# Linear attention's feature map: max(x, 0) + 1e-6 taken from PSUM behind the exp, min(exp, 1) added from SBUF

## The chip, the cores and the metric

The kernel runs on one core of a Trainium2 chip. The time is the device time of one execution in microseconds; the profiled execution has a span (first to last instruction) and its own time, which is a little longer. The core has five engines that run their own instruction streams and meet at semaphores: TensorE (PE), VectorE (DVE), ScalarE (ACT), GpSimd (POOL) and SyncE (SP, which issues DMAs here). Matmul results land in PSUM, in eight banks of 128 x 512 fp32; everything else lies in SBUF.

## The reference

Two blocks work on inputs of the same shapes (2048 tokens, 640 features, 32 heads of 20), and their outputs stand side by side. A is softmax attention, B linear attention:

```python
    def _A_ref(x, wqkv, wo):
        ...
        scores = jnp.einsum("bhqd,bhkd->bhqk", q, k) * (Dh ** -0.5)
        p = _softmax(scores, axis=-1)
        o = jnp.einsum("bhqk,bhkd->bhqd", p, v)
        ...
    def _B_ref(x, wqkv, wo):
        ...
        phi = lambda t: jnp.where(t > 0, t + 1, jnp.exp(t)) + 1e-6
        pq, pk = phi(q), phi(k)
        kv = jnp.einsum("bhsd,bhse->bhde", pk, v)
        z = jnp.einsum("bhsd->bhd", pk)
        num = jnp.einsum("bhqd,bhde->bhqe", pq, kv)
        den = jnp.einsum("bhqd,bhd->bhq", pq, z)[..., None] + 1e-6
        o = num / den
        ...
```

The feature map phi is the place of the change. It is computed as max(t, 0) + min(exp(t), 1) + 1e-6, which is the same for both signs of t.

## The kernel before

A is the large part. For each of 32 pairs of a query block (512 tokens) and a group of four heads, and each key tile of 128 tokens, PE makes the scores of four heads (matmuls `ps<-f_Qr,f_KT`), the exponential of them goes to SBUF, and PE multiplies it with V (`ps<-f_PT,f_V`). Most exponentials are ACT's: L1968 takes two PSUM banks at once (128 x 1024), 726 times. The others DVE makes in another way: L1828 clamps and rounds a bank to int16 (`f_Sr`), whose bits are read as bf16; POOL shifts them twice with INT64_ADD (L2039), and PE multiplies the three versions with V (`ps<-f_Sr,f_V` and `ps<-f_Sr,f_Vp`). PSUM bank 7 collects A's products with V; banks 1 to 4 take the scores for ACT in two pairs; the three auxiliary banks 0, 5 and 6 take everything else, DVE's scores and all of B.

B and the projections are put between A's work. B has two halves: for every 512 tokens K's features, V and their products (`kstep`, `vstep`, `kvstep`), then, behind a "turn", Q's features, the quotients and the output projection (`qstep`, `ndstep`, `trstep`, `ostep`). K's and Q's features come from `phi`, five banks per 512 tokens each, so 40 calls in all.

`phi` takes one auxiliary bank `b` with 512 columns. ACT writes exp of it to one of two SBUF buffers (`r1`, L1467); DVE does min(r1, 1) + 1e-6 in place (L1469), and then max(bank, 0) + r1 to the destination (L1471). Only after this is the bank given back (`self.abank.append(b)`). The exp of the next call but one waits for the same buffer.

The order of the instructions is no order of the source. A planner written in Python runs when the kernel is built: every engine has a clock, every operation a cost from a small formula (for DVE `_c_dve(n)` = 1.042 n + 68 ns, for L1469 0.95 n + 110), and what is ready first by these clocks is put into the engine's stream. On the chip each engine then runs its own stream in that fixed order and waits on semaphores where the data isn't ready. B's steps are paced by the share of A's exponentials that are placed. A change of a cost, or of the point at which a bank is given back, therefore moves instructions everywhere behind it.

Two more rules matter. An operation that reads a PSUM bank is booked as if it wrote it, so two readers of a bank follow each other (`op`, L118). And `turn` makes ACT and DVE wait, before Q's features begin, for everything that still uses buffers of the first half.

Of the kernel before, what the change touches and what calls it, by code (L numbers as in the profile page):

```python
# [7 lines left out]
BF16 = mybir.dt.bfloat16  # L8
# [4 lines left out]
ALU = mybir.AluOpType  # L13
# [730 lines left out]
def _c_dve(n):  # L744
    return 1.042 * n + 68
# [6 lines left out]
def _c_act(n):  # L752
    return 0.8333 * n + 50
# [27 lines left out]
class _Fast:  # L781
# [119 lines left out]
    def alloc(self):  # L901
        S, NT, NQC = self.S, self.NT, self.NQC
        self.KT = self.sb("f_KT", [128, N_GRP, S], BF16)
        self.V = self.sb("f_V", [128, NT, N_HEADS, 21], BF16)
        self.Vp = self.sb("f_Vp", [128, len(self.DKT), N_HEADS, 21], BF16)
        self.xT = self.sb("f_xT", [128, N_DC, S], BF16)
        self.wqp = self.sb("f_wqp", [128, _NP, N_DC, 128], BF16)
        zt = self.sb("f_zt", [128, 128], BF16)
        self.zt = zt[:]
        self.zr = zt[:].unsqueeze(1).broadcast_to([128, 2, 128])  # L910
        self.wq = self.sb("f_wq", [128, N_DC, D_MODEL], BF16)
        ar = self.sb("f_ar", [128, 20480], BF16)
        self.ar = ar
        nw = N_DC * D_MODEL
        self.wk = ar[:, 0:nw].rearrange("p (c n) -> p c n", c=N_DC)
        self.wv = ar[:, nw:2 * nw].rearrange("p (c n) -> p c n", c=N_DC)
        self.wB = ar[:, 0:2 * nw].rearrange("p (c n) -> p c n", c=N_DC)
        o = 2 * nw
        self.pk = ar[:, o:o + 2560].rearrange("p (t n) -> p t n", t=4)
        self.o = ar[:, o:o + 1280].rearrange("p (t n) -> p t n", t=2)  # L920
        self.oT = [ar[:, o + 1280 + 640 * k:o + 1920 + 640 * k] for k in range(2)]
        self.va = ar[:, o + 2560:o + 5248].rearrange("p (t h j) -> p t h j", t=4, j=21)
        self.pqT = ar[:, o + 2560:o + 5120].rearrange("p (c s) -> p c s", c=N_DC)
        o += 5248
        self.kvm = ar[:, o:o + 840].rearrange("p (c n) -> p c n", c=N_DC)
        self.kvacc = ar[:, o + 840:o + 2520].bitcast(F32).rearrange("p (c n) -> p c n", c=N_DC)
        self.oT += [ar[:, o + 840 + 640 * k:o + 1480 + 640 * k] for k in range(2)]
        self.wst0 = ar[:, o + 2432:o + 3712].rearrange("p (k c n) -> p k c n", k=2, c=N_DC)
        self.xn = ar[:, 2 * nw:2 * nw + 12 * D_MODEL].rearrange("p (t n) -> p t n", t=12)
        ee = ar[:, o + 2520:o + 2520 + 1024].rearrange("p (k n) -> p k n", k=2)  # L930
        self.er = {320: ee, 512: ee}
        o += 3712
        self.wkp = ar[:, o:o + 640 * _NP].rearrange("p (g c m) -> p g c m", g=_NP, c=N_DC)
        self.kq = [ar[:, o + 640 + 2048 * k:o + 640 + 2048 * (k + 1)] for k in range(2)]
        self.xB = [ar[:, o + k * 2560:o + (k + 1) * 2560].rearrange("p (c s) -> p c s", c=N_DC) for k in range(2)]
        assert o + 5120 <= 20480
        self.wo = self.sb("f_wo", [128, 7, D_MODEL], BF16)
        self.sq = self.sb("f_sq", [128, self.NSQ, 512], BF16)
        self.Qr = self.sb("f_Qr", [128, 4, 512], BF16)
        self.PT = self.sb("f_PT", [128, self.NPT, 512], BF16)  # L940
        self.xs = self.PT[:].rearrange("p t n -> p (t n)")[:, 4096:4096 + 4 * D_MODEL].rearrange("p (t n) -> p t n", t=4)
        self.Sr = self.sb("f_Sr", [128, self.NS, 4, 512], I16)
        self.T2 = self.sb("f_T2", [128, 512], BF16)
        self.OTn = self.sb("f_OTn", [128, 3 + self.NX, 512], BF16)
        self.OTd = self.sb("f_OTd", [128, 5, 512], BF16)
        self.Rt = self.sb("f_Rt", [128, 16 * self.NN], F32)
        self.stage = self.sb("f_st", [128, 4, 512], BF16)
        self.rd = self.sb("f_rd", [128, 2, 2, 24], F32)
        self.ident = self.sb("f_id", [128, 128], BF16)
        sm = self.sb("f_sm", [128, 8], F32)  # L950
        self.kb, self.km, self.gm = (sm[:, 2 * k:2 * k + 2] for k in range(3))
        self.warm, self.ones = sm[:, 6:7], sm[:, 7:8]
        self.kb16 = self.sb("f_kb16", [128, 2], BF16)
        self.g2 = self.sb("f_g2", [1, 2], F32)
        self.flag = self.sb("f_flag", [1, 1], I32)
        xf = self.xT[:].rearrange("p c s -> p (c s)")
        self.gt = xf[:, 5120:5120 + 4 * 1024].bitcast(F32).rearrange("p (k n) -> p k n", k=2)
# [498 lines left out]
    def phi(self, b, n, dst, res, key, extra=()):  # L1456
        k = self.brr % 2
        self.brr += 1
        src = self.ps[:, b, 0:n]
        r1 = self.er[n][:, k, 0:n]  # L1460
        rk = ("r1", n, k)
        prev = self.eru.get(k)
        self.eru[k] = key

        def ok():
            return prev is None or prev in self.done
        self.push("act", lambda e: e.activation(r1, src, AF.Exp), (("ps", b),), (rk,), _c_act(n), prio=0, ok=ok,  # L1467
                  after=lambda: self.push(
                      "dve", lambda e: e.tensor_scalar(r1, r1, 1.0, 1e-6, op0=ALU.min, op1=ALU.add), (rk,), (rk,),  # L1469
                      0.95 * n + 110, prio=0, after=lambda: self.push(  # L1470
                          "dve", lambda e: e.scalar_tensor_tensor(dst, src, 0.0, r1, op0=ALU.max, op1=ALU.add),  # L1471
                          (("ps", b), rk) + tuple(extra), (res,), _c_dve(n), prio=self.P5,
                          after=lambda: (self.done.add(key), self.abank.append(b)))))

    def b_steps(self):
        ps = self.ps
        sch = self.sch
# [123 lines left out]
        out.append(_Step(None, second, needs=allk, key="ld2"))  # L1601

        def turn(b):
            sch.barrier(("act", "dve"), tuple(("r1", 320, k) for k in range(2))
                        + tuple(("kva", c) for c in range(N_DC))
                        + tuple(("va", q) for q in range(6)) + tuple(("pk", q) for q in range(5)) + ("va1",))
        out.append(_Step(None, turn, needs=tuple(("kvm", c) for c in range(N_DC)), key="turn"))

        def qstep(tc, c, slot, needs):
# [886 lines left out]
```

## Time and profile before

| | |
|---|---|
| median of 3 runs | 718.65 us (718.63 to 719.19) |
| profiled execution | 718.41 us |
| its span | 716.7 us |
| granted TensorE clock, mean | 0.999 |

The page and the answers of the trace share their columns. A row of a group has the line, the engine, the operation, out<-in with shapes and the count; behind the bar stand the busy time of the group in us and the mean duration in ns; behind the second bar how long the engine was idle just before such an instruction, and what ended it. Since successive instructions of an engine overlap a little, the mean duration is longer than the step from one to the next. A row of the timeline begins with start and duration in us. Buffer numbers are left out of names. All of the planner's matmuls have one line, L166, that of the helper. `f_ar` is one large SBUF arena in which B's weights, inputs, K's and Q's features and the buffers r1 lie; `f_tt` is new with the change.

### The profile page before, as it was taken

The page shows a single profiled execution, that of the slowest core. Times are in us where ns is not written, and L with a number is a line of the kernel's source. Part 1 is how long each engine was busy: PE and PEld are TensorE (multiplying, and loading weights), DVE is VectorE, ACT ScalarE, POOL GpSimd, SP SyncE. Part 2 cuts the span into 40 slices and gives each one's busy share as a digit, 9 for nine tenths or more (in the row PEclk, how much of TensorE's full clock was granted, in tenths as well). Part 3 has the DMA queues.
Part 4 walks back from the last instruction along what each step waited for, and adds up shares of the span by engine and source line. Part 5 has one row for each costly group of instructions (what it writes and reads, how often), then busy time and mean ns, then how long its engine had stood idle before and what let it go on. Part 6 is the DMA issues. An engine that isn't in the chain of part 4 may idle for free.

```text
span 716.7 us, 25639 instructions
## 1 busy us (share of the span) xinstructions
PE 701.6 (98%) x11221; PEld 240.8 (34%) x11221; DVE 612.6 (85%) x1103; ACT 692.5 (97%) x774; POOL 329.7 (46%) x329
## 2 busy tenths in 40 slices
PE   8999999999899999999999999999999999999997
PEld 5423333333223333333332333333232333333333
DVE  6988888888888888887989887898888888999992
ACT  4789999999999999999999999999999999999996
POOL 6644354454535554245453357432444434444452
PEclk9999999999999999999999999999999999999999
DMA  9601010101340012011000112301020110010001
GB/s 267 105 18 36 12 31 9 40 12 30 88 100 7 22 33 60 10 24 35 7 11 10 34 25 71 78 14 36 8 55 25 47 28 6 26 28 7 28 16 39
DMA packets 46554, 27.59 MB, mean 38 GB/s; under 512 B 30842, under 2 KB 45882, under 8 KB 46442
## 3 DMA queue, kind: packets, MB, share of 16 engines
q1 hardware_dynamic: 43818, 23.98, 14.0%
q10 hardware_dynamic: 2624, 1.97, 0.9%
q8 instruction: 88, 1.44, 0.8%
q14 instruction: 24, 0.20, 0.1%
HBM read 8.40 MB, written 5.24 MB: 19 GB/s over the span
## 4 chain that ended last, share of the span: by engine, by line
ACT 58%; PE 36%; DVE 3%; POOL 2%; DMA 1%; issue 0%; ACTq 0%; DVEq 0%
ACT f_PT L1968 56%; PE ps L166 36%; POOL f_KT L1167 2%; ACT f_ar L1467 2%; DVE f_Sr L1828 1%; DMA f_ar<-in_A_wqkv_dram 1%; POOL f_V L1145 0%; DVE ps L2085 0%; PE ps L1046 0%; DVE f_ar L1471 0%; DVE f_PT L1419 0%; DVE f_ar L1469 0%; POOL f_Sr L2039 0%; DVE ps L2070 0%; DVE f_OTn L2079 0%
## 5 line engine op out<-in xcount | busy, mean ns | idle before, releaser
L1968 ACT ACTIVATE f_PT<-ps 128x1024 bf16<-128x1024 f32 x726 | 675.7, 1094 | 13.0 <-PE ps L166 12.3
L2039 POOL INT64_ADD f_Sr<-f_Sr x298 | 306.4, 1042 | 371.7 <-PE ps L166 343.1
L1828 DVE TENSOR_SCALAR f_Sr<-ps 128x512 int16<-128x512 f32 x596 | 402.2, 684 | 70.6 <-PE ps L166 64.2
L166 PE MATMUL ps<-f_Qr,f_KT 32*128 32x512 bf16 x2048 | 286.8, 384 | 7.3 <-ACT f_PT L1968 6.1
L166 PEld LDWEIGHTS ps<-f_Qr,f_KT 32*128 32x128 bf16 x2048 | 72.0, 91 | 256.2 <-ACT f_PT L1968 233.4
L166 PE MATMUL ps<-f_ar 128*32 128x512 bf16 (+6 forms) x3024 | 144.6, 295 | 0.7 <-DVE f_Sr L1828 0.3
L166 PE MATMUL ps<-f_PT,f_V 128*21 128x512 bf16 x1452 | 135.1, 383 | 0.1
L166 PE MATMUL ps<-f_Sr,f_V 128*21 128x512 bf16 x1192 | 106.9, 382 | 0.8 <-DVE f_T L2089 0.4
L166 PEld LDWEIGHTS ps<-f_ar 128*32 128x32 bf16 x3024 | 56.4, 95 | 58.0 <-issue 34.6
L166 PE MATMUL ps<-f_Sr,f_Vp 128*21 128x512 bf16 x596 | 57.5, 382 | 0.0
L166 PEld LDWEIGHTS ps<-f_PT,f_V 128*21 128x21 bf16 x1452 | 33.6, 90 | 46.2 <-issue 39.7
L166 PEld LDWEIGHTS ps<-f_Sr,f_V 128*21 128x21 bf16 x1192 | 26.5, 90 | 34.0 <-issue 24.7
L166 PE MATMUL ps<-f_ar,f_xT 128*32 128x160 bf16 x1280 | 34.8, 234 | 0.0
L166 PE MATMUL ps<-f_xT,f_ar 128*32 128x512 bf16 x400 | 30.8, 383 | 0.0
L166 PE MATMUL ps<-f_wo,f_OTd 128*32 128x512 bf16 (+5 forms) x608 | 30.6, 302 | 0.0
L166 PEld LDWEIGHTS ps<-f_ar,f_xT 128*32 128x32 bf16 x1280 | 22.8, 96 | 13.6 <-issue 9.5
L1471 DVE SCALAR_TENSOR_TENSOR f_ar<-ps,f_ar 128x512 bf16<-128x512 f32 x40 | 26.8, 671 | 0.2
L1467 ACT ACTIVATE f_ar<-ps 128x512 bf16<-128x512 f32 x40 | 26.5, 663 | 0.0
L1026 DVE CAST f_st<-ps 128x512 bf16<-128x512 f32 x35 | 23.9, 682 | 1.2 <-PE ps L166 0.9
L166 PE MATMUL ps<-f_xT,f_wq 128*32 128x512 bf16 x320 | 24.9, 383 | 0.0
L1469 DVE TENSOR_SCALAR f_ar<-f_ar 128x512 bf16<-128x512 bf16 x40 | 20.4, 509 | 3.7 <-ACT f_ar L1467 2.4
L2085 DVE STREAM_TRANSPOSE ps<-ps 128x512 f32<-128x512 f32 x31 | 22.4, 723 | 0.3 <-PE ps L166 0.2
(76 smaller groups left out, 278.2 us busy)
## 6 DMA issues: line engine op xcount, KB each, us to landing
out_dram<-f_st SPq DMA_DIRECT2D x35, 128.0 KB
f_ar<-in_B_wqkv_dram SPq DMA_DIRECT2D x15, 160.0 KB
f_OTd<-f_OTn SPq DMA_DIRECT2D x105, 20.0 KB
f_Qr<-f_sq SPq DMA_DIRECT2D x88, 20.0 KB
f_KT<-f_ar SPq DMA_DIRECT2D x22, 80.0 KB
f_ar<-in_A_wqkv_dram SPq DMA_DIRECT2D x1, 800.0 KB
f_ar<-in_A_wqkv_dram ACTq DMA_DIRECT2D x1, 800.0 KB
f_wq<-in_A_wqkv_dram ACTq DMA_DIRECT2D x1, 800.0 KB
```

The source lines that it names most:

```text
L166: lambda e: e.matmul(out, lhsT, rhs, start=start, stop=stop, tile_position=tp, skip_group_check=sgc),
L1026: (lambda e: e.tensor_copy(sl, ps[:, b, 0:w])), (("ps", b),), (res,),
L1167: self.push("pool", lambda e, g=g: e.tensor_copy(self.KT[:, g, :], self.kb16[:, 1:2].broadcast_to([128, self.S])), ("kb16",), tuple(("K", ...
L1467: self.push("act", lambda e: e.activation(r1, src, AF.Exp), (("ps", b),), (rk,), _c_act(n), prio=0, ok=ok, after=lambda: self.push("dve", ...
L1469: "dve", lambda e: e.tensor_scalar(r1, r1, 1.0, 1e-6, op0=ALU.min, op1=ALU.add), (rk,), (rk,),
L1471: "dve", lambda e: e.scalar_tensor_tensor(dst, src, 0.0, r1, op0=ALU.max, op1=ALU.add),
L1828: post = lambda: self.push("dve", lambda e: e.tensor_scalar(self.Sr[:, s, i, :], self.ps[:, b, :], 0.0, 32639.0 - self.PH[-1], op0=ALU.max ...
L1968: return _Op("act", lambda e: e.activation(self.PT[:, s0:s0 + n, :], ps[:, b0:b0 + n, :], AF.Exp, scale=math.log(2.0) / 128.0, bias=self.l ...
L2039: self.q["pool"].append(_Op("pool", lambda e: e.int64_add(v, v, inc), res, res, self.C64, self.C64 + 150, 0, self.seq, after))
L2085: self.push("dve", lambda e: e.transpose(ps[:, b, :], ps[:, b, :]), (), (("ps", b),), 630, prio=-1, ok=lambda: n == 0 or ("OTn", n - 1) in ...
```

## The change

```diff
--- before.py
+++ after.py
@@ alloc
+        self.tt = self.sb("f_tt", [128, 2, 512], BF16)
@@ phi
+        tt = self.tt[:, k, 0:n]
+        tk = ("tt", k)
+
         def ok():
             return prev is None or prev in self.done
+
+        def freed():
+            self.abank.append(b)
+            self.push("dve", lambda e: e.scalar_tensor_tensor(dst, r1, 1.0, tt, op0=ALU.min, op1=ALU.add),
+                      (tk, rk) + tuple(extra), (res,), _c_dve(n) + 100, prio=self.P5,
+                      after=lambda: self.done.add(key))
         self.push("act", lambda e: e.activation(r1, src, AF.Exp), (("ps", b),), (rk,), _c_act(n), prio=0, ok=ok,
                   after=lambda: self.push(
-                      "dve", lambda e: e.tensor_scalar(r1, r1, 1.0, 1e-6, op0=ALU.min, op1=ALU.add), (rk,), (rk,),
-                      0.95 * n + 110, prio=0, after=lambda: self.push(
-                          "dve", lambda e: e.scalar_tensor_tensor(dst, src, 0.0, r1, op0=ALU.max, op1=ALU.add),
-                          (("ps", b), rk) + tuple(extra), (res,), _c_dve(n), prio=self.P5,
-                          after=lambda: (self.done.add(key), self.abank.append(b)))))
+                      "dve", lambda e: e.tensor_scalar(tt, src, 0.0, 1e-6, op0=ALU.max, op1=ALU.add),
+                      (("ps", b),), (tk,), _c_dve(n), prio=0, after=freed))
@@ b_steps, turn
-            sch.barrier(("act", "dve"), tuple(("r1", 320, k) for k in range(2))
+            sch.barrier(("act", "dve"), tuple(("r1", w, k) for w in (320, 512) for k in range(2))
```

DVE's first operation of a call now reads the bank and writes max(x, 0) + 1e-6 to a new SBUF buffer `tt` (two of them); the bank is given back there. Its second one adds min(r1, 1) to it, with both inputs in SBUF, and is planned at 100 ns more. The exp on ACT is as before. The barrier at the turn names the buffers r1 under the width that is in use.

On DVE, from the first call of phi in the program on, there stood (line, operation, out<-in and width; `f_ar<-f_ar` and `f_ar<-ps,f_ar` are phi's two, `f_Sr<-ps` A's exponentials on DVE, `f_ar<-ps` with CAST B's V, and `f_T`, `f_OTn`, `f_Rt` belong to A's normalization):

```order
L1469 TENSOR_SCALAR f_ar<-f_ar 128x512
L1471 SCALAR_TENSOR_TENSOR f_ar<-ps,f_ar 128x512
L1828 TENSOR_SCALAR f_Sr<-ps 128x512
L1469 TENSOR_SCALAR f_ar<-f_ar 128x512
L1471 SCALAR_TENSOR_TENSOR f_ar<-ps,f_ar 128x512
L1828 TENSOR_SCALAR f_Sr<-ps 128x512
L1529 CAST f_ar<-ps 128x24x20
L1828 TENSOR_SCALAR f_Sr<-ps 128x512 x2
```

The same place of DVE's stream now, where the lines behind phi count seven more:

```order
L1479 TENSOR_SCALAR f_tt<-ps 128x512
L1474 SCALAR_TENSOR_TENSOR f_ar<-f_ar,f_tt 128x512
L1835 TENSOR_SCALAR f_Sr<-ps 128x512
L1479 TENSOR_SCALAR f_tt<-ps 128x512
L1474 SCALAR_TENSOR_TENSOR f_ar<-f_ar,f_tt 128x512
L1835 TENSOR_SCALAR f_Sr<-ps 128x512
L1536 CAST f_ar<-ps 128x24x20
L1835 TENSOR_SCALAR f_Sr<-ps 128x512 x2
```

The pairs are replaced one for one here and nothing else moves; each pair still stands closely together, ahead of the next exponential of A. From the third pair on the order differs.

On PE the streams part a little behind the third call. There stood (scores `f_Qr,f_KT`, A's products with V `f_Sr,f_V` and `f_PT,f_V`, and B's projections `f_ar`):

```order
L166 MATMUL ps<-f_Qr,f_KT 128x512 x3
L166 MATMUL ps<-f_PT,f_V 21x512 x4
L166 MATMUL ps<-f_Qr,f_KT 128x512 x3
L166 MATMUL ps<-f_Sr,f_V 21x512 x4
L166 MATMUL ps<-f_PT,f_V 21x512 x4
L166 MATMUL ps<-f_Sr,f_V 21x512 x4
L166 MATMUL ps<-f_Qr,f_KT 128x512 x3
L166 MATMUL ps<-f_PT,f_V 21x512 x4
L166 MATMUL ps<-f_Sr,f_V 21x512 x4
L166 MATMUL ps<-f_Qr,f_KT 128x512 x3
L166 MATMUL ps<-f_Sr,f_V 21x512 x4
L166 MATMUL ps<-f_ar 32x512 x4
```

The same place of PE's stream now:

```order
L166 MATMUL ps<-f_Qr,f_KT 128x512 x3
L166 MATMUL ps<-f_PT,f_V 21x512 x4
L166 MATMUL ps<-f_Sr,f_V 21x512 x4
L166 MATMUL ps<-f_Qr,f_KT 128x512 x3
L166 MATMUL ps<-f_PT,f_V 21x512 x8
L166 MATMUL ps<-f_Qr,f_KT 128x512 x3
L166 MATMUL ps<-f_Sr,f_V 21x512 x4
L166 MATMUL ps<-f_PT,f_V 21x512 x4
L166 MATMUL ps<-f_ar 32x512 x4
L166 MATMUL ps<-f_Qr,f_KT 128x512 x3
L166 MATMUL ps<-f_ar 32x512 x8
```

Both pieces begin with the first scores behind the point where the streams part. B's next projection stood behind the fourth group of scores and now stands behind the third, and the products with V have changed places around it.

At the end of PE's stream, on both sides of the last scores, there stood (`f_wo,f_OTd` and `f_wo,f_OTn` are A's output projection):

```order
L166 MATMUL ps<-f_wo,f_OTd 32x512 x4
L166 MATMUL ps<-f_wo,f_OTn 32x512 x4
L166 MATMUL ps<-f_Qr,f_KT 128x512 x2
L166 MATMUL ps<-f_Sr,f_V 21x512 x4
L166 MATMUL ps<-f_PT,f_V 21x512 x4
L166 MATMUL ps<-f_Qr,f_KT 128x512 x2
```

The same place of PE's stream now:

```order
L166 MATMUL ps<-f_wo,f_OTd 32x512 x8
L166 MATMUL ps<-f_wo,f_OTn 32x512 x4
L166 MATMUL ps<-f_Qr,f_KT 128x512 x2
L166 MATMUL ps<-f_Sr,f_V 21x512 x4
L166 MATMUL ps<-f_PT,f_V 21x512 x4
L166 MATMUL ps<-f_Qr,f_KT 128x512 x2
```

One block of the output projection is cut differently between the scores; everything from the last scores on is the same. ACT's stream has 726 exponentials of A and 40 of B in both.

## Prediction
> **What bounds the kernel now.** I read the page first: the busy times, the chain and the costliest groups.
>
> ```profile
> span 716.7 us, 25639 instructions
> PE 701.6 (98%) x11221; PEld 240.8 (34%) x11221; DVE 612.6 (85%) x1103; ACT 692.5 (97%) x774; POOL 329.7 (46%) x329
> ACT 58%; PE 36%; DVE 3%; POOL 2%; DMA 1%; issue 0%; ACTq 0%; DVEq 0%
> ...
> L1968 ACT ACTIVATE f_PT<-ps 128x1024 bf16<-128x1024 f32 x726 | 675.7, 1094 | 13.0 <-PE ps L166 12.3
> L2039 POOL INT64_ADD f_Sr<-f_Sr x298 | 306.4, 1042 | 371.7 <-PE ps L166 343.1
> L1828 DVE TENSOR_SCALAR f_Sr<-ps 128x512 int16<-128x512 f32 x596 | 402.2, 684 | 70.6 <-PE ps L166 64.2
> ...
> L1471 DVE SCALAR_TENSOR_TENSOR f_ar<-ps,f_ar 128x512 bf16<-128x512 f32 x40 | 26.8, 671 | 0.2
> L1467 ACT ACTIVATE f_ar<-ps 128x512 bf16<-128x512 f32 x40 | 26.5, 663 | 0.0
> ...
> L1469 DVE TENSOR_SCALAR f_ar<-f_ar 128x512 bf16<-128x512 bf16 x40 | 20.4, 509 | 3.7 <-ACT f_ar L1467 2.4
> ```
>
> ScalarE (ACT) is busy 97%, TensorE (PE) 98%, and 94% of the chain runs through these two. ACT's work is 726 exponentials of A's scores (L1968) and 40 of B's feature map (L1467). The 13.0 us of idle time before L1968 could be what is left to win, so I looked for it in the timeline of ACT, and then cut the span by stages.
>
> ```profile
> 49.52 155.29 ACT L1968 ACTIVATE f_PT<-ps 128x1024 bf16<-128x1024 f32 x169 [2.67 <-PE ps L166]
> 631.93 12.04 ACT L1968 ACTIVATE f_PT<-ps 128x1024 bf16<-128x1024 f32 x13 [0.27 <-PE ps L166]
> core 0: us, PE busy (x) PEld busy (x) DVE busy (x) ACT busy (x) POOL busy (x), PEclk, DMA share, GB/s
> 49.52:204.58 155.06, 152.48 (x2583) 52.60 (x2579) 131.89 (x230) 155.03 (x170) 75.45 (x75) 1.00 0.16 38
> 204.58:652.23 447.65, 442.88 (x6889) 145.27 (x6881) 392.07 (x697) 446.83 (x506) 195.60 (x198) 1.00 0.12 29
> 652.23:708.40 56.17, 55.53 (x838) 18.93 (x839) 43.98 (x85) 56.16 (x62) 30.58 (x30) 1.00 0.06 16
> 708.40:716.70 8.30, 4.17 (x114) 2.65 (x102) 4.92 (x16) 1.61 (x4) 0.00 (x0) 0.90 0.24 83
> ```
>
> All but 0.27 us of that idle time lies before 49.52 us. The second stage of the table, 204.58 to 652.23 us, runs from the first L1467 to the end of the last; nothing that the change touches lies before it. From 49.52 us until the last exponential ends (708.40) ACT never visibly rests. So the bound is ACT's instruction stream, and the time moves only if that stream starts later, is stretched, or if the last 8.30 us change.
>
> Stretching that the idle column does not show can be worked out. In the first stage 169 exponentials (170 records, one overhangs the edge) take 155.06 us: 0.9175 us each. An L1467 takes 0.48 us of the stream, by the starts here.
>
> ```profile
> 222.65 0.63 ACT L1467 ACTIVATE f_ar<-ps 128x512 bf16<-128x512 f32 x1
> 223.13 7.71 ACT L1968 ACTIVATE f_PT<-ps 128x1024 bf16<-128x1024 f32 x8
> 230.81 0.60 ACT L1467 ACTIVATE f_ar<-ps 128x512 bf16<-128x512 f32 x1
> ```
>
> The second stage holds 506 records, two of them overhanging, 40 of them L1467, so 464 exponentials: 464 x 0.9175 + 40 x 0.48 = 444.9 us against 447.65. **2.7 us of hidden lateness** lie in that stage. That is the most a change there can win, unless the exponentials get faster than in the first stage.
>
> **The change, part by part.** ACT keeps its 766 exponentials, and PE its matmuls but for one filler. On VectorE (DVE) 40 pairs are replaced. Old pair: L1469 and L1471, 20.4 + 26.8 = 47.2 us. The 509 ns mean of L1469 is no plain duration:
>
> ```profile
> L1469 DVE TENSOR_SCALAR f_ar<-f_ar x40: 251/294/1162, 205.3 to 652.5; 128x512 bf16<-128x512 bf16 x40
> 223.28 2.08 POOL L2039 INT64_ADD f_Sr<-f_Sr  x2 [0.23 <-PE ps L166]
> 223.31 1.16 DVE L1469 TENSOR_SCALAR f_ar<-f_ar 128x512 bf16<-128x512 bf16 x1
> ```
>
> Its median is 294 ns. At 223.31 us it began 0.03 us after an INT64_ADD of GpSimd (POOL) and took 1.16 us, as long as that add plus a little. Being blocked in this way costs 20.4 - 40 x 0.294 = 8.6 us in all, about 17 times half an add (0.52 us).
>
> The Trainium skill (SBUF — State Buffer, "Who interferes with whom") says that GpSimd and VectorE's second pair of ports share an exclusive lock; the 1.16 us above agrees. It also says that an instruction with two SBUF inputs contends with a GpSimd instruction that reads SBUF, while one with a single PSUM input does not. By it the new first instruction is free of the lock and the new second one is not; without that rule the blocked 8.6 us would go.
>
> New first instruction: PSUM to SBUF, 512 wide, like L1828: 40 x 0.684 = 27.4 us. New second one: two bf16 tensors in SBUF, a form the trace does not show. Lower bound 0.294 us (L1469 unblocked), upper bound 0.684 us and blocked by half an add every time (0.52). I take 0.671 from L1471, the same operation with two tensors, and the same 8.6 us of blocking, since POOL's adds stay: 26.8 + 8.6 = 35.4. Sum 62.8 us, **15.6 us more than before**; by the bounds 27.4 + 11.8 - 47.2 = 8.0 less, or 27.4 + 27.4 + 20.8 - 47.2 = 28.4 more.
>
> DVE has 447.65 - 392.07 = 55.6 us idle in that stage, so it does not become the bound. What counts is lateness against the order that the planner has fixed. It charged 1.198 us a pair and now 1.303; the trace gives 47.2/40 = 1.18 before, 62.8/40 = 1.57 now. What is queued behind the pair on DVE, mostly the L1828 that empty score banks for PE, comes 0.27 us later than planned, where it was 0.02 early. The cover for that:
>
> ```profile
> DVE f_Sr L1828 <- PE ps L166: 64.2, 228, 1.0
> 222.16 0.10 PEld L166 LDWEIGHTS ps<-f_Qr,f_KT 32*128 32x128 bf16 x3 [0.43 <-ACT f_PT L1968]
> ```
>
> DVE itself waits 228 times, 0.28 us each, and PE typically stands 0.43 us at its score matmuls until ACT has read the bank. A delay of 0.27 us costs ACT nothing as long as it meets one of these. It is not covered where a block comes on top:
>
> ```profile
> 458.82 42.97 ACT L1968 ACTIVATE f_PT<-ps 128x1024 bf16<-128x1024 f32 x46
> 501.69 0.59 ACT L1467 ACTIVATE f_ar<-ps 128x512 bf16<-128x512 f32 x1
> 459.11 1.08 DVE L1469 TENSOR_SCALAR f_ar<-f_ar 128x512 bf16<-128x512 bf16 x1 [0.24 <-ACT f_ar L1467]
> 460.05 0.39 PE L166 MATMUL ps<-f_Qr,f_KT 32*128 32x512 bf16 x3 [0.47 <-ACT f_PT L1968]
> ```
>
> A 1.08 us L1469 stands at the start of this run, in which 46 exponentials take 42.87 us instead of 42.2: 0.67 us lost. After the block at 223.31, eight take 7.68 us instead of 7.34 (rows above): 0.34 lost. Over the stage the 2.7 us of lateness against 8.6 us of blocking make at most 0.31 us per us. I count the 17 blocked pairs with their extra 0.27 us at this rate: 17 x 0.27 x 0.31 = **+1.4 us** (0 if covered as the other 23 are, +4.6 if each comes through in full).
>
> The bank: PE's bank was held for L1469 and L1471 (1.18 us), and now for the new first instruction alone (0.684). The planner knows it and starts other steps in it. PE waited for L1471 very little:
>
> ```profile
>   PEld ps L166: 0.4, 2
> ```
>
> I take **-0.4 us**, between 0 and the whole 2.7. The new tensor_scalar still stands behind the exp, as the old one did, since a read of a PSUM bank is booked as a write, so nothing overlaps that did not before. The wait added at the turn (ACT and DVE, on r1) is for work that K's masked sums have long needed: 0. The tail: the order after the last score matmuls is the same on PE and DVE, and B ends before it: 0.
>
> Sum: 718.41 (the profiled execution: 716.7 us of span and 1.7 around it) + 1.4 - 0.4 = **719.4 us**. The median of the runs is 718.65, 0.24 above the profiled one; a measurement of this kernel tells about 0.2% (1.4 us) from no change, so 717.2 to 720.1 is "the same".
>
> **The rivals.**
>
> *Slower: a blocked two-SBUF instruction makes PE late.* The place is DVE's queue behind the new second instruction; the price is the extra 0.27 us at each of 17 blocks, in full: +4.6 us, 723.0 us; half of it gives 720.7. It decides once block and lateness together exceed PE's 0.43 us, which half an add (0.52) does alone. For it speaks the run at 458.82; against it, that the old blocks cost 2.7 us in all at most. By the skill's rule above it can happen; without the lock it cannot.
>
> *Faster: the bank comes free early and outside the block.* Before, a blocked L1469 also kept PE's bank. If that, and not DVE's queue, made most of the 2.7 us, they go: 718.41 - 2.7 = 715.7 us, with half of it 717.1. For it: the bank is held 0.5 us less, 40 times, with three such banks. Against it: only 0.4 us of PE's waits name L1471, and many slow stretches of ACT hold no block.
>
> *The cheap case:* the second instruction runs in 0.294 us and is never blocked. DVE is relieved of 8.0 us, 8.0 x 0.31 = 2.5 us go, 715.9 us. Nothing in the trace shows a two-tensor instruction that fast.
>
> *A new order that is unlucky elsewhere.* The planner reshuffles PE from the third pair on; the visible stall at 631.93 shows that its plan leaves single gaps of 0.3 us. I count this as +-1 us within each case.
>
> **How the numbers follow.** Forecast (within 0.2%): 0.47. Slower rival: 0.31. Faster, by the bank 0.17 and by the cheap case 0.05: 0.22. The range reaches over most of both rivals, from 716.4 to 722.4 us; the forecast's own part of it is 717.2 to 720.1.
>
> **What would show it.** The new tensor_scalar at about 0.68 us with no long ones; the new scalar_tensor_tensor with a median near 0.67 and some records up to 1.7 that begin inside an INT64_ADD; DVE's busy time up by some 16 us; ACT's stream from the first L1467 to the last exponential within 1.5 us of 503.8 us. The forecast is wrong if that stream is longer by 2 us or more with PE waiting for L1828's successor (slower), or shorter by as much (faster), or if the last 8.3 us have changed.

## The result and the profile after

| | before | after |
|---|---|---|
| median | 718.90 us (7 runs, 718.58 to 719.94) | 723.91 us (7 runs, 722.86 to 728.15) |
| ratio | | 1.0075, 95% interval 1.0054 to 1.0096 |
| profiled execution, its span | 718.41, 716.7 us | 723.91, 722.2 us |

The change makes the kernel slower by 5.0 us. The page of the changed kernel, busy times, chain and the groups that answer to those of before:

```profile
span 722.2 us, 25638 instructions
PE 705.5 (98%) x11222; PEld 240.5 (33%) x11222; DVE 627.8 (87%) x1103; ACT 694.5 (96%) x774; POOL 335.7 (46%) x329
...
ACT 47%; PE 45%; DVE 6%; issue 1%; DMA 1%; POOL 1%; SPq 0%; DVEq 0%; ACTq 0%
...
L1975 ACT ACTIVATE f_PT<-ps 128x1024 bf16<-128x1024 f32 x726 | 678.2, 1091 | 16.2 <-PE ps L166 15.3
L2046 POOL INT64_ADD f_Sr<-f_Sr x298 | 312.4, 1064 | 372.3 <-PE ps L166 316.3
...
L1474 DVE SCALAR_TENSOR_TENSOR f_ar<-f_ar,f_tt 128x512 bf16<-128x512 bf16 x40 | 37.6, 940 | 0.3
...
L1479 DVE TENSOR_SCALAR f_tt<-ps 128x512 bf16<-128x512 f32 x40 | 27.4, 685 | 2.0 <-ACT f_ar L1477 1.1
```

DVE is busy 15.2 us more (612.6 before). ACT waits for PE 3.0 us more before its exponentials (12.3 before), and DVE and POOL, 5% of the chain before, now hold 7%. One row was not looked for: POOL's adds, which the change doesn't touch, take 312.4 us instead of 306.4. The durations of single instructions, in the view of one tile (minimum, median, maximum in ns), show both sides of a block. The last row is that of the adds before:

```profile
L1474 DVE SCALAR_TENSOR_TENSOR f_ar<-f_ar,f_tt x40: 642/693/1573, 205.8 to 659.4; 128x512 bf16<-128x512 bf16 x40
L2046 POOL INT64_ADD f_Sr<-f_Sr x298: 1030/1037/1467, 23.5 to 712.2; - x149
L2039 POOL INT64_ADD f_Sr<-f_Sr x298: 1032/1040/1180, 24.2 to 706.7; - x149
```

Unblocked, the new instruction takes 0.693 us. Its mean of 0.940 leaves 37.6 - 40 x 0.693 = 9.9 us of blocking; 17 of the 40 took over 0.9 us. The adds are held up in turn: their longest was 1180 ns before and is 1467 ns now.

Where the 5.5 us of span come from is read by stages: from the first call of phi to the last, from there to the end of the last exponential, and the tail (columns as before).

```profile
204.29:656.29 452.00, 446.11 (x6925) 145.79 (x6921) 408.53 (x701) 450.44 (x507) 204.24 (x201) 1.00 0.11 29
656.29:713.66 57.37, 56.09 (x798) 18.02 (x794) 42.81 (x81) 54.78 (x60) 28.05 (x27) 0.97 0.06 16
713.66:722.20 8.54, 4.40 (x118) 2.82 (x110) 4.92 (x16) 1.61 (x5) 0.00 (x0) 0.96 0.24 82
```

From the first L1467 to the end of the last exponential there were 503.81 us before (204.58 to 708.39), now 509.37: 5.56 us more. The tail is 0.2 us longer. So it is ACT's stream that is stretched, as the prediction's bound has it. The second row shows something else: TensorE's granted clock is 0.97 in the last 57 us, where it was 1.00. ACT's timeline there has three visible stalls:

```profile
656.29 0.60 ACT L1477 ACTIVATE f_ar<-ps 128x512 bf16<-128x512 f32 x1
656.77 1.96 ACT L1975 ACTIVATE f_PT<-ps 128x1024 bf16<-128x1024 f32 x2
659.34 3.05 ACT L1975 ACTIVATE f_PT<-ps 128x1024 bf16<-128x1024 f32 x3 [0.61 <-PE ps L166]
662.84 36.40 ACT L1975 ACTIVATE f_PT<-ps 128x1024 bf16<-128x1024 f32 x39 [0.44 <-PE ps L166]
700.43 13.23 ACT L1975 ACTIVATE f_PT<-ps 128x1024 bf16<-128x1024 f32 x14 [1.19 <-PE ps L166]
```

**The first kind of loss: blocks.** Ahead of the stall at 659.34 stand these rows of DVE, POOL and PE's weight loads:

```profile
655.06 1.33 DVE L1474 SCALAR_TENSOR_TENSOR f_ar<-f_ar,f_tt 128x512 bf16<-128x512 bf16 x1
656.32 0.68 DVE L1835 TENSOR_SCALAR f_Sr<-ps 128x512 int16<-128x512 f32 x1
656.92 0.70 DVE L2069 STREAM_TRANSPOSE f_OTn<-f_T 128x512 bf16<-128x512 bf16 x1
657.54 0.65 DVE L1835 TENSOR_SCALAR f_Sr<-ps 128x512 int16<-128x512 f32 x1
653.37 9.46 POOL L2046 INT64_ADD f_Sr<-f_Sr  x8
658.24 0.25 PEld L166 LDWEIGHTS ps<-f_ar 128*32 128x32 bf16 x16 [0.55 <-DVE f_Sr L1835]
```

The new instruction starts while POOL adds without a rest, and takes 1.33 us. Behind it in DVE's queue two L1835 empty score banks; PE needs the second bank for B's quotients and stands 0.55 us for it, the scores behind that come late, and ACT stands 0.61 us. The eight adds take 1.18 us each instead of 1.04.

**The second kind: TensorE's clock.** The 1.19 us at 700.43 have no block near them. In windows of the changed kernel there:

```profile
695.00:696.00 1.00, 0.93 (x7) 0.18 (x3) 1.00 (x3) 1.00 (x2) 0.00 (x0) 1.00 0.41 87
696.00:697.00 1.00, 0.47 (x5) 0.11 (x3) 1.00 (x3) 1.00 (x2) 0.00 (x0) 1.00 0.21 44
697.00:698.00 1.00, 0.93 (x8) 0.31 (x11) 1.00 (x3) 1.00 (x2) 0.00 (x0) 0.84 0.00 0
698.00:701.00 3.00, 3.00 (x26) 0.48 (x18) 2.03 (x4) 1.81 (x3) 2.44 (x3) 0.50 0.03 5
701.00:702.00 1.00, 1.00 (x18) 0.25 (x15) 0.68 (x2) 1.00 (x2) 1.00 (x2) 0.96 0.00 0
```

PE rests 0.67 us in the three us from 695 (0.07 + 0.53 + 0.07), and then the clock is granted at one half, from the middle of 697 on, for 0.32 + 3.0 + 0.08 = 3.4 us (a window at 0.84 is at a half for 0.32 of it). Just ahead, PE has nothing but scores to make, and those wait for ACT:

```profile
694.62 1.39 PE L166 MATMUL ps<-f_Qr,f_KT 32*128 32x512 bf16 x7
696.54 1.36 PE L166 MATMUL ps<-f_Qr,f_KT 32*128 32x512 bf16 x6 [0.53 <-ACT f_PT L1975]
697.83 1.46 PE L166 MATMUL ps<-f_Sr,f_V 128*21 128x512 bf16 x12
```

In the new order 13 scores stand in a row here and B's small matmuls, which lay between them before, are spent. The twelve products behind take 1.46 us; twelve take 0.83 at full clock elsewhere in these traces. In the kernel before, this point looked so:

```profile
689.00:690.00 1.00, 0.71 (x4) 0.20 (x4) 1.00 (x3) 1.00 (x3) 0.00 (x0) 1.00 0.00 0
690.00:691.00 1.00, 0.85 (x34) 0.55 (x34) 1.00 (x3) 1.00 (x3) 0.00 (x0) 1.00 0.00 0
691.00:692.00 1.00, 0.93 (x37) 0.44 (x25) 1.00 (x3) 1.00 (x2) 0.00 (x0) 1.00 0.00 0
```

PE rested 0.51 us in three (many small matmuls stand in the second and third), and kept its clock. But the rest alone doesn't make the drop. Two other places of the changed kernel's own trace:

```profile
186.00:189.00 3.00, 1.96 (x24) 0.50 (x18) 2.33 (x4) 3.00 (x5) 0.00 (x0) 1.00 0.31 95
541.00:544.00 3.00, 2.33 (x28) 0.91 (x32) 3.00 (x8) 3.00 (x4) 0.00 (x0) 1.00 0.14 44
```

PE rests 1.04 and 0.67 us in these three us, as much or more, and the clock is full there and behind. What else has to come together is not shown.

The 3.4 us at half clock are called a clock drop below. Of runs without a profile only the mean clock is known, and it is a rough sign: the tail alone, at 0.90 for 8.3 us before, takes 0.001 of it. Of the changed kernel's seven runs, the two at 0.999 or more took 722.86 and 723.17 us; the five at 0.998 or less, where one or more drops are to be supposed (the profiled run is one), 723.63 to 728.15. So, by two runs, the change costs some **4 us without the clock drop**, and the drop, in most runs, adds about 1 us to the median.

### The profile page after: what moved, and what is told of

Read it like the earlier page. It is cut to its first block, busy times and chain, and to the rows that moved or that the text cites. A ratio compares the mean times of both kernels' runs of the same rounds, so it can differ in the third digit from the quotient of the medians.

```text
span 722.2 us, 25638 instructions
## 1 busy us (share of the span) xinstructions
PE 705.5 (98%) x11222; PEld 240.5 (33%) x11222; DVE 627.8 (87%) x1103; ACT 694.5 (96%) x774; POOL 335.7 (46%) x329
## 4 chain that ended last, share of the span: by engine, by line
ACT 47%; PE 45%; DVE 6%; issue 1%; DMA 1%; POOL 1%; SPq 0%; DVEq 0%; ACTq 0%
ACT f_PT L1975 45%; PE ps L166 44%; DVE f_Sr L1835 2%; ACT f_ar L1477 1%; DVE f_ar L1474 1%; DVE f_tt L1479 1%; DMA f_PT<-in_A_x_dram 1%; POOL f_Sr L2046 1%; PE ps L1047 0%; DVE ps L2092 0%; DVE f_PT L1420 0%; DVE f_st L1027 0%; DVE f_sq L1258 0%; DVE f_OTn L2069 0%; DVE ps L2077 0%
## 5 line engine op out<-in xcount | busy, mean ns | idle before, releaser
L2046 POOL INT64_ADD f_Sr<-f_Sr x298 | 312.4, 1064 | 372.3 <-PE ps L166 316.3
L1835 DVE TENSOR_SCALAR f_Sr<-ps 128x512 int16<-128x512 f32 x596 | 401.6, 683 | 67.4 <-PE ps L166 62.5
L166 PEld LDWEIGHTS ps<-f_ar 128*32 128x32 bf16 x3024 | 54.5, 95 | 56.8 <-issue 35.1
L166 PEld LDWEIGHTS ps<-f_Sr,f_V 128*21 128x21 bf16 x1192 | 26.8, 90 | 36.0 <-issue 22.9
L1474 DVE SCALAR_TENSOR_TENSOR f_ar<-f_ar,f_tt 128x512 bf16<-128x512 bf16 x40 | 37.6, 940 | 0.3
L166 PE MATMUL ps<-f_ar,f_xT 128*32 128x160 bf16 x1280 | 34.8, 234 | 0.0
L1479 DVE TENSOR_SCALAR f_tt<-ps 128x512 bf16<-128x512 f32 x40 | 27.4, 685 | 2.0 <-ACT f_ar L1477 1.1
L1477 ACT ACTIVATE f_ar<-ps 128x512 bf16<-128x512 f32 x40 | 26.8, 671 | 0.0
```

The source lines that it names most:

```text
L166: lambda e: e.matmul(out, lhsT, rhs, start=start, stop=stop, tile_position=tp, skip_group_check=sgc),
L1474: self.push("dve", lambda e: e.scalar_tensor_tensor(dst, r1, 1.0, tt, op0=ALU.min, op1=ALU.add), (tk, rk) + tuple(extra), (res,), _c_dve(n ...
L1479: "dve", lambda e: e.tensor_scalar(tt, src, 0.0, 1e-6, op0=ALU.max, op1=ALU.add),
L1835: post = lambda: self.push("dve", lambda e: e.tensor_scalar(self.Sr[:, s, i, :], self.ps[:, b, :], 0.0, 32639.0 - self.PH[-1], op0=ALU.max ...
L2046: self.q["pool"].append(_Op("pool", lambda e: e.int64_add(v, v, inc), res, res, self.C64, self.C64 + 150, 0, self.seq, after))
```

## The experiments

Six theories were in play. At first: L, the pair is later than the planner was told; O, the new order itself; B, blocks at the lock between DVE and POOL. Then, for what a block does: M, the mean length of the pair counts; P, the peaks on DVE; G, POOL's adds are held up and A's products come late. Lags below are the start of each call of phi against the first call, compared with e5, for kernels that have its order to the instruction; they are taken from the profiled runs, where every drop comes later than the last call.

**e1: the new instructions in the old order.** The plan is made with the old costs, inputs and outputs, and the new pair is emitted.

```diff
+ "dve", lambda e: e.tensor_scalar(tt, src, 0.0, 1e-6, ...), (rk,), (rk,), 0.95 * n + 110, real=((("ps", b),), (tk,)), ...
+     "dve", lambda e: e.scalar_tensor_tensor(dst, r1, 1.0, tt, ...), (("ps", b), rk) + extra, (res,), _c_dve(n), real=...
```

> The new pair of instructions in the old order of every engine: the planner is given the old costs and the old point at which the bank is free, and only the instructions' own waits follow the new reads and writes. Theory L (lateness: the pair takes 15 us more of VectorE and everything behind it is late): about 723.5 us, as the change. Theory O (order: the new plan itself has worse gaps, whatever the instructions take): about 719 us, as before. Theory B (blocking by GpSimd's adds alone): 722 to 724, since the blocked second instruction is in it.

721.23 us, ratio 1.0028 (1.0018 to 1.0038). The instructions alone cost 2.3 us in the order of before; the new one stands there at 34.8 us (870 ns), the adds at 309.7. No theory had this time: it lies between O's 719 and the 722 to 724 of B and L. Most runs show no clock drop here (mean clock below 0.999 in two of eight), and the loss is there without it. In the new order the same instructions cost some 4 us without the drop, so the order adds some 1.7 us to what they cost; through which rows is not shown.

**e2: the second instruction alone made short.** It becomes tensor_scalar, one SBUF input, in after's order.

```diff
- e.scalar_tensor_tensor(dst, r1, 1.0, tt, op0=ALU.min, op1=ALU.add)
+ e.tensor_scalar(dst, r1, 1.0, 1e-6, op0=ALU.min, op1=ALU.add)
```

> The changed kernel in its own order, but the second instruction is a tensor_scalar of r1 alone (min with 1, plus 1e-6), so max(x, 0) is left out of the feature map. It should take 0.29 us instead of 0.69 when not blocked, and is still blocked by GpSimd's adds. Theory L: VectorE is relieved of some 16 us, so 719 to 720 us. Theory O: 723 us or more. Theory B: 722 to 723.5, the blocks being as long as before.

719.73 us, 1.0027 (1.0006 to 1.0047). It is still blocked (median 295 ns, mean 514), but the adds are back at 305.3 us, and the last call lags 0.39 us. Six of its twelve runs show the clock drop; the other six took 718.3 to 719.1. This is L's time and a miss for B as it was put (722 to 723.5): a block alone, when the instruction is short and hardly delays the adds, costs almost nothing. So B is taken apart below.

**e3 and e4: a POOL that doesn't read SBUF.** The adds become memsets of the same tile, in after (e3) and in before (e4).

```diff
- v = ....bitcast(I64);  e.int64_add(v, v, inc)
+ v = ....bitcast(I32);  e.memset(v, 0)
```

> The changed kernel in its own order, with each INT64_ADD of GpSimd replaced by a memset of the same tile (1024 words of 32 bits, about as long), which reads nothing; the shifted versions of A's rounded exponentials are left out. Theory B: the second instruction loses its long records (mean from 940 to about 690 ns) and the time falls to 719 us or less. Theory L: VectorE gets back the 9.9 us of blocking out of 15, so about 720.5. Theory O: 723.5.

> The kernel before with the same memsets in place of the adds; the shifted versions of A's rounded exponentials are left out. L1469 shares two ports with GpSimd, so a writer alone can still block it. Theories L and B: 717.5 to 718.9, by how much of the 8.6 us of blocking goes; Theory O: 718.9. The difference to the changed kernel with memsets tells what is left of the change without GpSimd's reads: 0 by theory B, 1 to 2 us by theory L, 5 us by theory O.

e3 718.97 us, 1.0004 (0.9995 to 1.0014); e4 718.12, 0.9990 (0.9981 to 0.9999). In the page of e3 the pair is free:

```profile
L2046 POOL MEMSET f_Sr<- 128x1024 int32 x298 | 273.4, 953 | 406.5 <-PE ps L166 349.4
...
L1474 DVE SCALAR_TENSOR_TENSOR f_ar<-f_ar,f_tt 128x512 bf16<-128x512 bf16 x40 | 27.1, 678 | 0.3
```

With nothing that reads on POOL, the same long pair in the same order takes 0.1 us more than before. That speaks for B and against O. Against e4, the comparison that was set up, 0.85 us is left, where B expected 0 and L 1 to 2, so L isn't settled by it. And the memsets are also shorter than the adds (953 against 1064 ns). So the next pair of runs took the lock away on DVE's side. In e4 the old L1469 is blocked as ever (22.5 us, 564 ns) though POOL only writes. The Trainium skill (SBUF — State Buffer, "Who interferes with whom") says just this: an instruction with two SBUF inputs contends with a GpSimd instruction that reads, one in a two-port mode with any. Both rows agree, though no row says in which mode L1469 runs.

**e5 and e6: the lock taken away on DVE's side.** The first instruction writes the destination, the second is a transpose of other data, 512 wide (e5) or 736 (e6).

```diff
- e.scalar_tensor_tensor(dst, r1, 1.0, tt, op0=ALU.min, op1=ALU.add)
+ e.transpose(tt_flat[:, 0:512], self.xT[:, 0, 0:512])
- e.tensor_scalar(tt, src, 0.0, 1e-6, op0=ALU.max, op1=ALU.add)
+ e.tensor_scalar(dst, src, 0.0, 1e-6, op0=ALU.max, op1=ALU.add)
```

> The changed kernel in its own order with GpSimd's adds, but the second instruction is a 128x512 transpose of a bf16 tile in SBUF: one source, about 0.70 us, like L2062, which never varies. The first instruction writes straight to the destination, and min(exp, 1) is left out. Theory B (the lock, in either direction): 719 us, as with memsets; adds back at 305 us of busy time. Theory M (the longer mean time of the pair): 720.5, since 0.70 without blocks is 10 us less than the 37.6 of the change.

> As e5_unblocked with a transpose of 736 columns, about 0.93 us each time: as long as the changed kernel's second instruction is in the mean (0.94), but never blocked and blocking nothing. min(exp, 1) is left out. Theory M: 723.5 us. Theory P (only the long single blocks on VectorE count, the ordinary ones are covered): 719 to 720.5. Theory G (what counts is that a long second instruction keeps GpSimd's adds waiting): 719 to 720.

e5 718.57 us, 1.0008 (0.9995 to 1.0022); e6 719.75, 1.0016 (1.0004 to 1.0028). The transposes take 698 and 930 ns in the mean and 712 and 946 at most, and the adds 305.4 and 304.9 us. Without the clock drop e5's runs took 717.96 to 718.58 us and e6's 718.29 to 719.04: 40 times 0.23 us more, as much as the changed kernel's mean adds, cost about 0.4 us. M falls, and with it L, which goes by the same mean; so does the bad order by itself: after's order with a free pair is as fast as before while the clock holds.

**e8: peaks on DVE alone.** A 256 wide transpose (431 ns), then the short instruction of e2, which is blocked.

```diff
+ e.transpose(self.tt[:, k, 0:256], self.xT[:, 0, 0:256])
+ e.tensor_scalar(dst, r1, 1.0, 1e-6, op0=ALU.min, op1=ALU.add)
```

> The short second instruction of e2_short_second (tensor_scalar on r1, blocked by the adds, hardly blocking them), with a transpose of 256 columns ahead of it (about 0.44 us, never blocked). VectorE's time for a pair is then that of the change, blocks included, but the adds are held up for 0.2 us at most. max(x, 0) is left out. Theories M and P: 723 to 724. Theory G: 720 to 721.

720.52 us, 1.0031 (1.0020 to 1.0043); 720.00 to 720.52 without the drop. The short instruction takes 0.254 us unblocked here, so blocks are 18.0 - 40 x 0.254 = 7.8 us; the adds take 305.4. The last call lags 1.37 us. The time lies in G's range and outside M's and P's 723 to 724, but e5's runs without the drop are 1.4 us or more faster with adds just as long: P has a share, but not all.

**e9: late adds alone.** e5's free pair, and on POOL one short add of scratch ahead of the first add behind a pair.

```diff
+ w = self.tt[:, 1, 0:256].bitcast(I64);  e.int64_add(w, w, 0)
  return e.int64_add(v, v, inc)
```

> e5 (after's order, lock-free pair: the first instruction writes the destination, the second is a 128x512 transpose of other data, 0.70 us; so phi lacks its min(exp, 1)), and on GpSimd one short INT64_ADD (256 bf16 of scratch) ahead of the first add that follows a pair: 28 of them. Nothing on VectorE is blocked; only the adds come later, as the long two-input instruction makes them in the changed kernel (312.4 us busy against 305.4 in e5). Theory G (adds held up make the products with V late): median 1 to 3 us above e5's 718.6, so 719.6 to 721.6, with TensorE's weight loads waiting on GpSimd more than in e5. Rival P (only VectorE's own blocked peaks count): 718.0 to 719.0, as e5. In both, single runs 1.2 to 1.8 us longer where the mean clock is below 0.999.

721.57 us, 1.0043 (1.0029 to 1.0057). Its page:

```profile
L2058 POOL INT64_ADD f_Sr<-f_Sr x298 | 305.1, 1039 | 244.5 <-PE ps L166 208.8
...
L2057 POOL INT64_ADD f_tt<-f_tt x28 | 8.2, 291 | 125.1 <-PE ps L166 105.3
```

8.2 us of delay on POOL, where the changed kernel has 312.4 - 305.4 = 7.0, and nothing else, and the last call lags 1.45 us. All six runs have a mean clock of 0.998 or less, so part of the 3.0 us over e5 is clock. At a like clock, e9's four runs at 0.998 took 720.97 to 721.66 us and e5's three at 0.997 and 0.998 took 719.94 to 720.05: 0.9 to 1.7 us, as the lag says. G has a share too. PE's weight loads wait 12.6 us for POOL in 44 places (e5: 6.5 in 26; the changed kernel: 10.9 in 42). Such waits alone prove little: e3 has 10.6 in 44 and lags 0.52 us.

**e10: both.** e8's pair and e9's adds in one kernel.

> e9 and e8 in one kernel, in after's order: the first instruction writes the destination, the second is a 128x256 transpose of other data and then min(exp, 1) + 1e-6 from SBUF to SBUF (short, but blocked by GpSimd's adds), and on GpSimd one short INT64_ADD of scratch ahead of the first add behind a pair (28). The max(x, 0) is overwritten, so phi lacks it. If the loss is the sum of VectorE's blocked peaks and GpSimd's late adds: the last call of phi starts 2.0 to 3.2 us later than in e5, measured from the first (e8 1.37, e9 1.45, the changed kernel 2.72), and the runs without a clock drop take 721.5 to 723.2. If the two share the same cover (the larger counts): 1.4 to 1.8 us, and 719.8 to 721.0. Runs with a mean clock below 0.999 are 1.2 to 1.8 us longer, and are the larger part.

722.58 us, 1.0049 (1.0035 to 1.0062), as the sum expected; 721.64, 722.02 and 722.58 without the drop. The last call lags 2.37 us; e8's and e9's together make 2.82, and the changed kernel's lag is 2.72. The two add up, less a little cover that they share. The changed kernel's blocks are larger (9.9 us against 18.8 - 40 x 0.252 = 8.7 here), which fits the rest of its loss but was not tried apart.

**c6a and c6b: another second instruction.** phi is also min(exp(x), max(x, 0) + 1), which takes one operation with two inputs (the 1e-6 is left out). c6a keeps after's order; c6b is planned by the shorter cost.

```diff
- e.scalar_tensor_tensor(dst, r1, 1.0, tt, op0=ALU.min, op1=ALU.add)   # _c_dve(n) + 100
+ e.tensor_tensor(dst, r1, tt, op=ALU.min)                             # c6b: 0.52 * n + 68 + 150
- e.tensor_scalar(tt, src, 0.0, 1e-6, op0=ALU.max, op1=ALU.add)
+ e.tensor_scalar(tt, src, 0.0, 1.0, op0=ALU.max, op1=ALU.add)
```

> After's order to the instruction, but phi = min(exp(x), max(x, 0) + 1) (1e-6 left out): the second instruction is a tensor_tensor min with both inputs in SBUF. If it runs faster than the scalar_tensor_tensor (0.42 us or less unblocked against 0.69), DVE gives up 40 x 0.27 = 10.8 us against the changed kernel and GpSimd's adds are held up less: median 718.3 to 720.5, between e2 (719.7) and e5 (718.6); blocks of 5 to 8 us stay. If it takes 0.69 too: 723 to 724, as the changed kernel. Theory O (the order's long run of 13 score matmuls drops the clock): about half of its runs show a mean clock below 0.999 and are 1.2 to 1.8 us longer.

> The same two instructions as c6a, the second planned at 0.52 n + 218 ns, so in another order, whose longest run of score matmuls is 7. Theory O: hardly a run with a mean clock below 0.999, and a median of 717.5 to 719.0. If the clock drop has nothing to do with the long run: about half the runs are 1.2 to 1.8 us longer, as in c6a. If any new order costs by itself: over 720.

The new instruction in c6b, in the view of its tile:

```profile
L1474 DVE TENSOR_TENSOR f_ar<-f_ar,f_tt x40: 361/427/1126, 205.6 to 654.0; 128x512 bf16<-128x512 bf16 x40
```

It takes 0.427 us unblocked, not 0.693, and is blocked for 24.2 - 40 x 0.427 = 7.1 us. c6a: 721.31 us, 1.0033 (1.0021 to 1.0046), over what was expected, because eight of its twelve runs show the clock drop; the other four took 719.74 to 719.92. They stand in steps by their mean clock: 719.8 at 1.000, 721.3 to 721.5 at 0.997 to 0.998, 723.1 to 723.9 at 0.993, as if for none, one and more stretches of 3.4 us. The blocks, expected at 5 to 8 us, are 26.6 - 40 x 0.426 = 9.6 us, almost the changed kernel's 9.9; what is gone is 0.27 us of each pair and most of the adds' delay (307.4 us), and with it all but 0.57 us of the lag. c6b: 718.99 us, 0.9999 (0.9991 to 1.0008), the time of before; no run is above 719.67, and the two with a mean clock of 0.998 are no longer than the others.

**e11: the changed kernel's instructions in c6b's order.**

```diff
- ... _c_dve(n) + 100, prio=self.P5,
+ ... 0.52 * n + 68 + 150, prio=self.P5,
```

> The changed kernel's two instructions (min and add in one scalar_tensor_tensor, 0.69 us unblocked, blocked beyond) in c6b's order to the instruction. If c6b is as fast as before by its shorter second instruction: its 40 x 0.27 us and GpSimd's late adds come back, 720.5 to 723.0. If by its order: 718.7 to 719.7, as c6b. Clock: if the drop follows the late stream and not the order alone, some runs fall below a mean of 0.999 and are over 1 us longer, which no run of c6b was.

722.82 us, 1.0054 (1.0040 to 1.0068); all five between 722.23 and 723.07. c6b is fast by its instruction: 3.8 us lie between the two kernels, whose orders are the same. Windows of e11 at the place where after loses its clock:

```profile
695.00:696.00 1.00, 0.59 (x7) 0.10 (x3) 1.00 (x4) 1.00 (x3) 0.00 (x0) 1.00 0.00 0
696.00:697.00 1.00, 0.88 (x15) 0.31 (x15) 1.00 (x3) 1.00 (x3) 0.04 (x1) 1.00 0.00 0
697.00:700.00 3.00, 3.00 (x41) 0.72 (x33) 2.17 (x4) 3.00 (x4) 3.00 (x4) 1.00 0.02 5
```

It rests 0.53 us there and keeps its clock, late as it is. None of its five runs is over 1 us longer than the others. So the loss without the drop goes with the instruction, and whether the clock drops goes in the main with the order.

**c3: the plan told the true cost.** The second instruction is planned 260 ns above the plain cost, about its measured mean.

```diff
- ... _c_dve(n) + 100, prio=self.P5,
+ ... _c_dve(n) + 260, prio=self.P5,
```

> The changed kernel with its second instruction planned at its measured mean (260 ns above c_dve instead of 100), so that nothing is late against the plan on average; longest run of score matmuls 7. Theory L (lateness against the plan): median 719.5 to 721.5. Theories B, P and G (the blocks and the held-up adds come whatever was planned, since they fall on single pairs): 721.5 to 723.5, that is the changed kernel's runs without the clock drop. Theory O: hardly a run below a mean clock of 0.999.

725.68 us, 1.0088 (1.0075 to 1.0101): a miss for every theory. L expected a gain and there is a loss, and O hardly a run below 0.999 where all five are. Its windows show two clock drops, one of them here:

```profile
674.00:675.00 1.00, 0.47 (x6) 0.10 (x3) 1.00 (x4) 1.00 (x2) 0.00 (x0) 1.00 0.21 60
675.00:676.00 1.00, 0.70 (x7) 0.19 (x4) 1.00 (x3) 1.00 (x2) 0.00 (x0) 0.94 0.00 0
676.00:679.00 3.00, 3.00 (x25) 0.45 (x22) 2.32 (x4) 2.51 (x3) 2.09 (x3) 0.50 0.00 0
```

Its longest row of scores is 7, so the row of 13 isn't what the clock answers to. PE rests here too (0.53 + 0.30 us in two us). Why this order also loses 2.2 us more than after between the first call and the last (454.19 us, 452.00 in after) stays open.

**c1: min on GpSimd.** In before, L1469 goes to POOL and is planned there, so that DVE has no SBUF pair at all.

```diff
- "dve", lambda e: e.tensor_scalar(r1, r1, 1.0, 1e-6, ...), (rk,), (rk,), 0.95 * n + 110, ...
+ "pool", lambda e: e.tensor_scalar(r1, r1, 1.0, 1e-6, ...), (rk,), (rk,), _c_pool(n), ...
```

> The kernel before, replanned, with min(exp, 1) + 1e-6 done by GpSimd in place instead of VectorE's L1469; VectorE keeps the one instruction from PSUM. VectorE is relieved of 20 us and nothing shares ports with two sources; GpSimd gets 40 x 0.6 us, and the bank is held a little longer where an add is in front. Theories B, M and P: the hidden 2.7 us of ACT's stream shrink, 716 to 718.5. If banks held longer matter more: 719 to 721.

1072.74 us, 1.4923 (1.4903 to 1.4942), far from both expectations. Two rows of the view of waits (total us, times, longest):

```profile
POOL f_ar L1469 <- issue: 144.9, 20, 7.8
POOL f_Sr L2039 <- issue: 139.8, 23, 6.4
```

The instruction itself takes 1.94 us there, against 0.294 on DVE. Worse is that POOL stands 7.2 us ahead of it and 6.1 ahead of the next add, for no work that the profile counts. POOL's sequencer (POOLq) shows what stands there:

```profile
L1469 POOLq MODIFY_POOL_CONFIG  x48: 1/10/14, 204.8 to 970.4; - x48
L2039 POOLq MODIFY_POOL_CONFIG  x48: 11/11/11, 226.8 to 992.0; - x48
```

The kernel before has two of these, at its start. Here two stand at each of the 48 changes from one instruction to the other; the first is at 204.8 us, and the first L1469 begins at 212.7. The Trainium skill (GPSIMD Engine Reference, "2. Architecture") gives some 6 us for the first call to freshly loaded code on this engine, with no instruction in the profile. That the engine's configuration is changed each time is shown; that the gaps are the loading fits them, but no row shows the loading itself.

## Why the prediction was wrong

Predicted were 719.4 us with a range up to 722.4; the median is 723.91. The mechanism is in part the slower rival's (DVE's queue behind a blocked pair), in part one that no case held (POOL's adds held up), with a clock drop that no case held either.

- **The bound** was right: ACT's stream from the first L1477 on is 5.56 us longer; with a start 0.29 us earlier and a tail 0.24 longer that is the span's 5.5.
- **DVE's pair**: 62.8 us were predicted, 27.4 + 37.6 = 65.0 came. The first instruction is exact, the second 27.7 unblocked (26.8) and 9.9 blocked (8.6). DVE's busy time rose by 15.2 us (15.6). The rows of the pair came as they were forecast, with records up to 1.57 us. The sign of being wrong came too: the stream is longer by more than 2 us, and PE's weight loads wait 15.9 us for L1835 (13.7 for L1828 before) and 10.9 for POOL (5.9).
- **The term that failed is the +1.4 us**, "17 blocked pairs with their extra 0.27 us" at a rate of 0.31 us per us. The number of blocked pairs was right, 17, but some 4 us were lost without the clock drop. Two things were left out. The rate was taken from the old L1469 and applied to the increase alone, as if DVE were the only engine that a block delays. But a block has two sides: the old instruction was gone in 0.29 us, and left the adds at 306.4 us; the new one takes 0.69 us and delays them by 7.0 us against e5, and a delay of this size alone (8.2 us in e9) is a lag of 1.45 us. The blocks on DVE alone (e8) are a lag of 1.37 us. And blocks that follow each other aren't covered by PE's wait for ACT, 0.43 us in the row shown and 234.6 us in 595 places, 0.39 each, over the trace: around the three between 652 and 661 us stand stalls of 0.61 and 0.44 us, where e5 has none.
- **The bank, -0.4 us**, fits: e5, with the bank given back early and no lock, took 717.96 to 718.58 us while its clock held, 0.3 to 0.9 below 718.9. But e5 has none of the old blocks either, so the bank's own share isn't shown. Its median, with the drop in five runs of twelve, is no different from before.
- **The tail, 0**: 0.2 us.
- **The unlucky order, "+-1 us within each case"**, was wrong in kind. The order of after loses almost nothing by itself while the clock holds (e3, e5); with the blocks in it, it costs some 1.7 us more than the old order (e1). And it leaves PE without other work for some us near 695. Of all runs in this order, 45 of 85 over nine kernels have a mean clock below 0.999 (13 of 91 runs of before, taken beside them), and in the five of the nine profiles that hold a drop it lies between 695 and 702 us.
- **The rivals.** "Slower" gave 723.0 us, which is what the changed kernel's two runs with a full clock took (722.86, 723.17); its price, 0.27 us at each of 17 blocks in full, is no measured one, and the sum agrees in part by luck. It also leaves the adds out. The chance it had, 0.31, was too small: its point of decision, half an add (0.52 us) against PE's 0.43 us, was met on the page, and the argument against it (the old blocks cost 2.7 us at most) came from an instruction less than half as long (0.294 us against 0.693). "Cheap" and "faster" fell: nothing was blocked less.

## What to carry to other kernels

When an instruction takes a lock that another engine needs, price both sides: how long it can be blocked, and how long it blocks the other, by what each engine has queued behind. A two-input instruction from SBUF beside a busy GpSimd is worth avoiding, or making short: min as a plain tensor_tensor (0.43 us) gave 3.8 us back at the same order. And where a planner reorders, look at the places where TensorE has a single kind of work left that waits for another engine: the clock drop of this order fell at such a place, and its 3.4 us of half clock cost some 1.5 us (c6a: 719.8 against 721.3 to 721.5).

## What the hardware showed unexpectedly

**The clock.** It fell to one half behind rests of PE of only 0.67 us in three us (after, e8, e9, e10), stayed there 3.4 us, and fell in some runs and not in others of the same kernel: e5's profiled run rests as long (691 to 694: 0.25 + 0.40 + 0.02) and keeps its clock. Rests of 0.51 to 0.53 us near the same point (before, c6b, e11) kept it in these profiles, though e1's lost its clock behind 0.44, and rests of 0.67 and 1.04 us elsewhere in the changed kernel's trace kept it. So no amount of rest divides the two, and what trips the clock stays open. It isn't bound to phi either: e4's profile lost it at 189 us, ahead of the first call, and that run took the median time of its kernel (718.12). The Trainium skill (TensorE: Matmul & The Clock Gate, "Part 1: The HAM clock gate") speaks of a free-running activity window of about 3.4 us and of two clock states, one half of the other: the length, the half and the chance from run to run agree. By its table the clock falls after an idle window; here PE was busy some four fifths of the time before, and the measurement decides.

**Two-input instructions.** Of the same size and types, scalar_tensor_tensor took 0.693 us and tensor_tensor 0.427, both with two bf16 inputs in SBUF.
